# The products of a recurrence tile in three runs by array shape, with rank and table products moved to the end of a step

## The chip, the cores and the metric

One core of one Trainium2 chip. The metric is the device time of one execution in microseconds, the median of several runs.

## The reference

Three stages, one after the other, all in float32:

```
# 1. gated linear attention: 4 batches, 8 heads, 768 steps, 48 features
f = sigmoid(f_logit)
state = f[t] * state + outer(k[t], v[t])
y[t] = q[t] @ state
# 2. mixture of experts on y as 3072 tokens of 384: 8 experts, the best one alone
logits = x @ w_gate + modality_bias[modality_id]
e = argmax(logits); weight = softmax(logits)[e]
out = weight * (relu(x @ w1[e]) @ w2[e])           # 384 -> 1024 -> 384
# 3. gated linear unit, 384 -> 1536 -> 384
out = (sigmoid(x @ w_gate) * (x @ w_val)) @ w_out
```

## The kernel before, in words

Stage 1 goes over 24 tiles of 128 tokens (6 chunks of each of 4 batches, batches in turn, so tile i is chunk i // 4 of batch i % 4). Inside a tile the recurrence is done as matrix products over the 128 tokens; between chunks a state of 48 x 48 per head is carried on. The loop at L1245 has one step per tile and two more; step i works on several tiles at once, and the order in which it calls its parts is the order of every engine's queue (the schedule is by hand). The parts, with the name that the text uses for their products on TensorE:

- **k** (`att_k`, L951): four transposes of the decayed keys of tile i, copied to `kt` by ACT. Not in the last chunk.
- **a** (`att_a`, L962): eight products of 48 rows, keys times queries, into two PSUM banks; `att_m` (L972) masks them on DVE into `am`.
- **c** (`prep_c`, L916): eight products into 64 columns each, the running sums of the log decays of tile i+2. `prep_e` (L929) turns them into `r` and `g` by two exponentials on ACT, and `prep_mul` (L938) makes keys `kT` (DVE) and queries `qT` (POOL, in some tiles DVE) of them. `prep_l` (L907) makes the log decays of tile i+3 on ACT, `limit_f` (L903) limits the logits of tile i+4.
- **x** (`att_x`, L1037): four products that turn the result of tile i-2 back to one token per partition, with the router's logits beside it; ACT copies the rows, DVE sums the logits.
- **u** (`att_u`, L978): eight products of 64 columns, the state's update; DVE carries the state on in `state_steps`, and ACT copies it to `s_blk` in `att_s` (L1002).
- **ys** and **y** (`att_y`, L1009): tile i-1's output. ys are four products of the carried state with the queries (L1015; not in chunk 0, that is tiles 0 to 3), y are eight products of 64 columns of `am` with v (L1021), into the same PSUM bank; ACT copies it to `yT`.

float32 products run in two passes, so the timeline counts two instructions for each of the products of a, c, x, u, ys and y; a transpose is one.

Before the change a step's order on TensorE is k, a, (put), c, (rank), x, u, ys, y. PSUM: `ps_mm` has three banks, which a (two) and c (one) use in turn; `ps_o` has two, which u and yT use in turn; `ps_t` has two for k and x, and one for the routing's small products.

Routing goes by groups of tiles, ROUTE at L42: (0, 4), (4, 4), (8, 4), (12, 4), and so on. When x of a group's last tile is done, a chain of small DVE operations (`route_a`, L243) is put into `chains`; `tick` (L221) issues the next operation of the chains, and is called at places spread over a step; `drain` issues all that are left. One step later `att_r` (L1063) drains, runs the **rank** products (`route_rank`, L267) and puts in a second chain: positions (`route_pos`), counts (`route_cum`) and weights (`route_weight`), and for each tile of the group two marks (`mark`, L306). One step after that `put_table` (L325) drains, and runs the **table** products ("put") of the marks, two for each tile; `store_rows` (L1079) sends the group's rows to memory. With groups of four tiles this is in steps 6, 10, 14, 18 (rank) and 7, 11, 15, 19 (put and store).

SP's queue holds the loads (`load_f`, `load_kq`, `load_v` at the start of a step), the stores of rows, and, around the steps of CONV, loads and stores of the weights that are converted from 64 to 32 bits on ACT and DVE. The loads of a step are for tiles i+3 to i+5.

Stage 2 follows in slots of 256 tokens (`slot32` with float32 products, then `half_slot` and `slot` with split ones), stage 3 after it.

Of the kernel before, what the change touches and what calls it, by code (L numbers as in the profile page):

```python
# [41 lines left out]
ROUTE = ((0, 4), (4, 4), (8, 4), (12, 4), (16, 2), (18, 4), (22, 2))  # L42
CUM = len(ROUTE) % 2
CONV = (3, 7, 11, 15)
GROUP = (0, 6, 1, 2)
STAGED = (3, 7)
PADS = (320, 160, 352, 96)
# [13 lines left out]
def kernel(  # L61
# [181 lines left out]
    def route_a(logits_ps, bias, n, to):  # L243
        shp = [P, n, E]
        lg = small.tile(shp, F32, tag="lg", name="lg")
        nc.vector.tensor_tensor(out=lg, in0=logits_ps, in1=bias, op=ALU.add)
        yield
        mx = small.tile([P, n], F32, tag="mx", name="mx")
        nc.vector.tensor_reduce(out=mx, in_=lg, axis=AX.X, op=ALU.max)
        yield  # L250
        nc.vector.tensor_tensor(out=lg, in0=lg, in1=bc3(mx, shp, 2), op=ALU.subtract)
        ez = small.tile(shp, F32, tag="ez", name="ez")
        nc.scalar.activation(out=ez, in_=lg, func=AF.Exp)
        yield
        sc = small.tile(shp, F32, tag="sc", name="sc")
        w8b = bc3(w8, shp, 1)
        nc.vector.scalar_tensor_tensor(out=sc, in0=lg, scalar=0.0, in1=w8b, op0=ALU.is_ge, op1=ALU.mult)
        yield
        first = small.tile([P, n], F32, tag="first", name="first")
        nc.vector.tensor_reduce(out=first, in_=sc, axis=AX.X, op=ALU.max)  # L260
        yield
        oh = small.tile(shp, BF16, tag="oh", name="oh", bufs=3)
        nc.vector.tensor_tensor(out=oh, in0=w8b, in1=bc3(first, shp, 2), op=ALU.is_equal)
        to.update(oh=oh, ez=ez)
        yield

    def route_rank(oh, c, n, count=False):  # L267
        ps = ps_t.tile([P, n + count, E], F32, tag="lg", name="rank", bufs=1)
# [77 lines left out]
    def route_cum(oh, c, c_new, n):  # L346
        if n > 2:
            total = small.tile([P, E], F32, tag="total", name="total")
            nc.vector.tensor_reduce(out=total, in_=oh.rearrange("p n e -> p e n"), axis=AX.X, op=ALU.add)
            yield  # L350
            nc.vector.tensor_tensor(out=cum[c_new], in0=cum[c], in1=total, op=ALU.add)
            yield
        for j in range(n if n <= 2 else 0):
            nc.vector.tensor_tensor(out=cum[c_new], in0=cum[c if j == 0 else c_new], in1=oh[:, j], op=ALU.add)
            yield
# [650 lines left out]
                at = slice(64 * j, 64 * j + D)  # L1006
                nc.scalar.copy(out=s_blk[b][at, :, at], in_=s_sum[b][at])

    def att_y(i):  # L1009
        c, b = i // B, i % B  # L1010
        (am, _), qT, vt = st.pop(("am", i)), st.pop(("qT", i)), st.pop(("v", i))
        ps = ps_o.tile([P, 4, P], F32, tag="o", name="yT")
        if c:
            for pr in range(4):
                nc.tensor.matmul(  # L1015
                    out=ps[:, pr, :], lhsT=s_blk[b][:, pr, :], rhs=qT[:, pr, :], start=(pr == 0), stop=False
                )
        for pr in range(4):
            for j in range(2):
                h = 2 * pr + j  # L1020
                nc.tensor.matmul(  # L1021
                    out=ps[64 * j:64 * j + 64, pr, :], lhsT=vt[:, h * D:h * D + 64], rhs=am[:, 4 * j + pr, :],
                    start=(c == 0 and pr == 0), stop=(pr == 3),
                )
        yT = ap2.tile([P, 4, P], F32, tag="yT", name="yT")
        nc.scalar.copy(out=yT, in_=ps)
        st["yT", i] = yT
# [35 lines left out]
    def att_r(i):  # L1063

        drain()
        first_i, n = group_of[i]
        c = ROUTE.index((first_i, n)) % 2
        got = st.pop(("oh", first_i))
        oh = got["oh"]
        rank = route_rank(oh, c, n, i == NE - 1)  # L1070
        steps = (
            route_pos(oh, rank, n, first_i, late_at(first_i, n)),
            route_cum(oh, c, 1 - c, n), route_weight(got["ez"], st["rows", first_i], n),
        )
        if i == NE - 1:
            return rank[:, n], steps
        chains.append(turns(*steps))

    def store_rows(i):  # L1079
        first_i, n = group_of[i]  # L1080
        nc.sync.dma_start(
            out=xd[first_i * P:(first_i + n) * P, :].rearrange("(j p) f -> p j f", p=P),
            in_=st.pop(("rows", first_i))[:, 0:n],
        )


    def general(flag):
        with tc.If(flag != 0), ExitStack() as gctx:
# [53 lines left out]
            with tc.For_i(0, NTOK, P) as r0:  # L1142
                row = gp.tile([P, ROW], F32, name="grow", tag="grow")
                nc.sync.dma_start(out=row[:, 0:DM], in_=xg_d[bass.ds(r0, P), :])
                mi = gp.tile([P, 2], I32, name="gmi", tag="gmi")
                nc.sync.dma_start(out=mi, in_=modality[bass.ds(r0, P), :])
                m1 = gp.tile([P, 1], F32, name="gm1", tag="gm1")
                m0 = gp.tile([P, 1], F32, name="gm0", tag="gm0")
                nc.vector.tensor_copy(out=m1, in_=mi[:, 0:1])
                nc.vector.tensor_scalar(out=m0, in0=m1, scalar1=-1.0, scalar2=1.0, op0=ALU.mult, op1=ALU.add)  # L1150
                bi = gp.tile([P, 1, E], F32, name="gbi", tag="gbi")
                nc.vector.tensor_scalar(out=bi[:, 0], in0=bias_b[:, 0, :], scalar1=m0, scalar2=None, op0=ALU.mult)
                nc.vector.scalar_tensor_tensor(
                    out=bi[:, 0], in0=bias_b[:, 1, :], scalar=m1, in1=bi[:, 0], op0=ALU.mult, op1=ALU.add
                )
                pos_i = gp.tile([P, 1], I32, name="gpi", tag="gpi")
                nc.vector.tensor_copy(out=pos_i, in_=pos_f)
                ps = ps_t.tile([P, 3, P], F32, tag="t", name="gxT")
                for c in range(3):
                    nc.tensor.transpose(ps[:, c, :], row[:, c * P:(c + 1) * P], ident)  # L1160
                xt = gp.tile([P, 3, P], F32, name="gxt", tag="gxt")
                nc.vector.tensor_copy(out=xt, in_=ps)
                lg = ps_t.tile([P, 1, E], F32, tag="lg", name="glg", bufs=1)
                for c in range(3):
                    nc.tensor.matmul(out=lg[:, 0], lhsT=xt[:, c, :], rhs=wn[:, c, :], start=(c == 0), stop=(c == 2))
                got = {}
                run(route_a(lg, bi, 1, got))
                oh, ez = got["oh"], got["ez"]
                rank = route_rank(oh, CUM, 1)
                nc.gpsimd.tensor_copy(out=row[:, DM + 1:ROW].bitcast(I32), in_=pos_i)  # L1170
                at = [gp.tile([P, 1], F32, name=f"gat{x}", tag=f"gat{x}") for x in range(2)]
                run(route_pos(oh, rank, 1, to=at))
                g_row = gp.tile([P, 2, HI], F32, name="grw", tag="grw")
                g_place = gp.tile([P, P], F32, name="gpl", tag="gpl")
                nc.vector.tensor_scalar(out=g_row, in0=iota_hi, scalar1=at[1], scalar2=None, op0=ALU.is_equal)
                pos_t = gp.tile([P, 1], F32, name="gpt", tag="gpt")
                nc.vector.tensor_scalar(out=pos_t, in0=pos_f, scalar1=-float(MID), scalar2=None, op0=ALU.add)
                nc.vector.tensor_scalar(
                    out=g_place, in0=iota_lo, scalar1=at[0], scalar2=pos_t, op0=ALU.is_equal, op1=ALU.mult
                )  # L1180
                put = ps_t.tile([HI, 2, P], F32, tag="lg", name="gput", bufs=1)
                for half in range(2):
                    nc.tensor.matmul(
                        out=put[:, half], lhsT=g_row[:, half], rhs=g_place, start=(half == 0), stop=(half == 1)
                    )
                nc.vector.tensor_tensor(out=table, in0=table, in1=put, op=ALU.add)
                nc.vector.tensor_scalar(out=pos_f, in0=pos_f, scalar1=float(P), scalar2=None, op0=ALU.add)
                run(route_cum(oh, CUM, CUM, 1))
                run(route_weight(ez, row.rearrange("p (o f) -> p o f", o=1), 1))
                nc.sync.dma_start(out=xd[bass.ds(r0, P), :], in_=row)  # L1190
# [49 lines left out]
    def ticking(steps):  # L1240
        for _ in steps:
            tick()

    to_store = due = to_put = None
    for i in range(NT + 2):  # L1245
# [9 lines left out]
            load_v(i + 3)  # L1255
        if to_store is not None and to_store != NE - 1:
            store_rows(to_store)
        if i < NT:
            att_k(i)
            att_a(i)  # L1260
# [36 lines left out]
        if i < NT:  # L1297
            state = att_u(i)
            if i == 0:
                keep_warm(1)  # L1300
        if 0 <= i - 1 < NT:
            att_y(i - 1)
        if i == NT - 1:
            gps = ps_t.tile([1, P], F32, tag="lg", name="gps", bufs=1)
# [462 lines left out]
```

## Time and profile before

| what | value |
|---|---|
| median of 3 runs | 879.07 us (875.2 to 879.09) |
| the profiled execution's own time | 878.71 us |
| its span | 877.0 us |
| TensorE busy over the span | 97% |
| DVE, ACT, POOL busy over the span | 54%, 44%, 28% |
| mean granted TensorE clock | 0.991 |

The span runs from the first to the last instruction of the execution; the device time has some 1.7 us around it. Busy shares are means over stages with different limits. The recurrence's loop takes about the first fifth of the span. A step is read from TensorE's k to the next step's k.

### The profile page before, as it was taken

Reading aid. Unit: us, or ns where it says so; the run is one execution under the profiler, and the core shown is the slowest. Engines: PE = TensorE matmul, PEld = TensorE weight load, DVE = VectorE, ACT = ScalarE, POOL = GpSimd, SP = SyncE. Lnnn points to the kernel's source line nnn. Section 1 sums busy time; section 2 is a strip of 40 time slices with the busy share of each in tenths; the row PEclk is TensorE's granted clock in tenths of the full one; section 3 lists DMA queues with packets and bytes.
Section 4 is the critical chain, followed back from the end, with each engine's and each line's share of the span. In section 5 each row is a group of like instructions: output and inputs, shape, how many; then the busy total and the mean of one; then the engine's idle time right before and its main releaser. Section 6 shows DMA issues by size and latency. Waiting matters only on the chain.

```text
span 877.0 us, 15315 instructions
## 1 busy us (share of the span) xinstructions
PE 853.0 (97%) x5802; PEld 762.9 (87%) x5802; DVE 476.8 (54%) x1036; ACT 389.2 (44%) x804; POOL 249.8 (28%) x321
## 2 busy tenths in 40 slices
PE   7999999999999999999999999999999999999995
PEld 6888888777999999999888888888888888888885
DVE  5777778475987979976335334333423433442221
ACT  5866675225866656656432322232322332223222
POOL 5744443113445665564630200020020001002002
PEclk8999999999999999999999999999999999999998
DMA  9566653864989979976202021011012002000000
GB/s 324 177 219 232 217 171 123 332 242 149 336 302 327 330 270 321 333 260 226 80 10 64 27 47 35 1 55 37 18 46 46 19 1 64 10 0 37 1 1 36
DMA packets 52273, 121.15 MB, mean 138 GB/s; under 512 B 21018, under 2 KB 33318, under 8 KB 52192
## 3 DMA queue, kind: packets, MB, share of 16 engines
q1 hardware_dynamic: 47200, 105.10, 35.6%
q0 software_dynamic: 4992, 15.00, 4.8%
q8 instruction: 47, 0.77, 0.4%
q14 instruction: 34, 0.28, 0.1%
HBM read 96.44 MB, written 20.11 MB: 133 GB/s over the span
## 4 chain that ended last, share of the span: by engine, by line
PE 69%; DVE 4%; issue 1%; ACT 1%; POOL 0%; POOLq 0%; DVEq 0%; ACTq 0%
PE gv L1595 11%; PE gv L1596 11%; PE gv L1594 11%; PE y L735 8%; PE o L1619 6%; PE o L1617 6%; PE o L1618 6%; PE h L659 3%; PE h L656 3%; PE h L657 3%; DVE cvt L850 2%; DVE al L389 1%; DVE hl L663 1%; PE xT L403 0%; DVE bl L389 0%
## 5 line engine op out<-in xcount | busy, mean ns | idle before, releaser
L1605 DVE TENSOR_TENSOR sg<-sg,gv 128x256 f32<-128x256 f32 (+1 forms) x145 | 60.2, 415 | 209.3 <-PE gv L1596 209.3
L1606 ACT CAST gh<-sg 128x256 fp32r<-128x256 f32 (+1 forms) x145 | 58.7, 405 | 191.6 <-DVE sg L1605 191.6
L1625 POOL DMA_INDIRECT out_dram<-raw,tok x24 | 23.6, 984 | 375.5 <-ACT raw L1622 369.3
L1607 DVE TENSOR_TENSOR gl<-sg,gh 128x256 fp32r<-128x256 f32 (+1 forms) x145 | 64.3, 443 | 68.2 <-ACT gh L1606 68.2
L1604 ACT ACTIVATE sg<-gv 128x256 f32<-128x256 f32 (+1 forms) x145 | 55.2, 381 | 94.7 <-PE gv L1596 92.6
L393 POOL DMA_INDIRECT xg<-xd,ids x24 | 36.5, 1523 | 62.9 <-PE xT L403 38.9
L662 ACT ACTIVATE hh<-h 128x256 fp32r<-128x256 f32 x80 | 30.9, 386 | 42.7 <-PE h L659 42.0
L663 DVE SCALAR_TENSOR_TENSOR hl<-h,hh 128x256 fp32r<-128x256 f32 x80 | 33.3, 419 | 21.8 <-ACT hh L662 18.2
L1596 PE MATMUL gv<-oddh,al 128*128 128x512 f32 (+1 forms) x120 | 44.3, 369 | 0.0
L1595 PE MATMUL gv<-oddl,ah 128*128 128x512 f32 (+1 forms) x120 | 44.3, 369 | 0.0
L1594 PE MATMUL gv<-oddh,ah 128*128 128x512 f32 (+1 forms) x120 | 44.1, 367 | 0.0
L1596 PE MATMUL gv<-oddh,bl 128*128 128x512 f32 x108 | 42.5, 394 | 0.0
L1596 PE MATMUL gv<-evenh,bl 128*128 128x512 f32 x108 | 42.5, 393 | 0.0
L1595 PE MATMUL gv<-oddl,bh 128*128 128x512 f32 x108 | 42.4, 393 | 0.0
L1595 PE MATMUL gv<-evenl,bh 128*128 128x512 f32 x108 | 42.4, 393 | 0.0
L945 POOL TENSOR_TENSOR qT<-kq,g 128x512 f32<-128x512 f32 x19 | 24.4, 1283 | 62.9 <-ACT g L935 47.8
L1596 PE MATMUL gv<-evenh,al 128*128 128x512 f32 x108 | 42.3, 391 | 0.0
L1595 PE MATMUL gv<-evenl,ah 128*128 128x512 f32 x108 | 42.2, 391 | 0.0
L1594 PE MATMUL gv<-evenh,ah 128*128 128x512 f32 x108 | 42.0, 389 | 0.0
L1594 PE MATMUL gv<-evenh,bh 128*128 128x512 f32 x108 | 42.0, 389 | 0.0
L1594 PE MATMUL gv<-oddh,bh 128*128 128x512 f32 x108 | 42.0, 389 | 0.0
L975 DVE TENSOR_TENSOR am<-a,causal 128x512 f32<-128x512 f32 x48 | 31.2, 683 | 12.5 <-PE a L969 12.5
(365 smaller groups left out, 2487.8 us busy)
## 6 DMA issues: line engine op xcount, KB each, us to landing
raw<-in_w_dram SPq DMA_DIRECT2D x48, 768.0 KB, 5.8
kq<-in_att_kq_dram SPq DMA_DIRECT2D x24, 512.0 KB, 5.4
cvr<-in_w_glu_dram SPq DMA_DIRECT2D x14, 768.0 KB, 7.4
raw<-wd SPq DMA_DIRECT2D x7, 768.0 KB, 5.3
f<-in_att_fv_dram SPq DMA_DIRECT2D x24, 200.0 KB, 5.6
v<-in_att_fv_dram SPq DMA_DIRECT2D x24, 200.0 KB, 2.5
x<-yd SPq DMA_DIRECT2D x12, 386.0 KB, 3.4
xd<-rows SPq DMA_DIRECT2D x5, 772.0 KB
```

Source lines behind the costliest of these rows:

```text
L663: nc.vector.scalar_tensor_tensor(out=hl, in0=ps, scalar=0.0, in1=hh, op0=ALU.max, op1=ALU.subtract)
L735: nc.tensor.matmul(out=ps, lhsT=lhs[:, ts], rhs=rhs[:, fs], start=(g == 0 and part == 0), stop=(g == 7 and part == 2))
L1594: nc.tensor.matmul(out=ps[:, ns], lhsT=hi[:, sl], rhs=xh[:, c, ns], start=(c == 0), stop=False)
L1595: nc.tensor.matmul(out=ps[:, ns], lhsT=hi[:, sl], rhs=xl[:, c, ns], start=False, stop=False)
L1596: nc.tensor.matmul(out=ps[:, ns], lhsT=lo[:, sl], rhs=xh[:, c, ns], start=False, stop=(c == 2))
L1604: nc.scalar.activation(out=sg[:, sl], in_=pss[0][:, to], func=AF.Sigmoid)
L1605: nc.vector.tensor_tensor(out=sg[:, sl], in0=sg[:, sl], in1=pss[1][:, to], op=ALU.mult)
L1606: nc.scalar.copy(out=gh[:, sl], in_=sg[:, sl])
L1607: nc.vector.tensor_tensor(out=gl[:, sl], in0=sg[:, sl], in1=gh[:, sl], op=ALU.subtract)
L1617: nc.tensor.matmul(out=ps, lhsT=gh[:, ts], rhs=hi[:, fs], start=(f == 0), stop=False)
L1618: nc.tensor.matmul(out=ps, lhsT=gh[:, ts], rhs=lo[:, fs], start=False, stop=False)
L1619: nc.tensor.matmul(out=ps, lhsT=gl[:, ts], rhs=hi[:, fs], start=False, stop=(f == 11))
```

## The change

For steps 0 to 17 (GROUPED) the loop has a body of its own, with the same operations in another order. On TensorE: k, then ys of tile i-1 (split off `att_y` as `att_ys`), x of tile i-2; then a; then y of tile i-1, c of tile i+2, u; then, in steps 9, 13 and 17 (PUT), the table products, and in steps 6, 10 and 14 the rank products. The table products thus come three steps behind the rank products, and without a drain. `store_rows` is called at the end of steps 8, 12 and 16. The exponential of the logits is taken out of `route_a` and is issued by `att_r` (`route_exp`), on ACT ahead of `prep_e`. From step 18 on the order is the old one. No product, copy or transfer is added or left out.

```diff
+GROUPED = 17
+PUT = (9, 13, 17)
...
@@ route_a
-        ez = small.tile(shp, F32, tag="ez", name="ez")
-        nc.scalar.activation(out=ez, in_=lg, func=AF.Exp)
...
-        to.update(oh=oh, ez=ez)
+        to.update(oh=oh, lg=lg)
...
+    def route_exp(lg, n):
+        ez = small.tile([P, n, E], F32, tag="ez", name="ez")
+        nc.scalar.activation(out=ez, in_=lg, func=AF.Exp)
+        return ez
...
-    def att_y(i):
+    def att_ys(i):
         c, b = i // B, i % B
-        (am, _), qT, vt = st.pop(("am", i)), st.pop(("qT", i)), st.pop(("v", i))
+        qT = st.pop(("qT", i))
         ps = ps_o.tile([P, 4, P], F32, tag="o", name="yT")
         if c:
             for pr in range(4):
                 nc.tensor.matmul(
                     out=ps[:, pr, :], lhsT=s_blk[b][:, pr, :], rhs=qT[:, pr, :], start=(pr == 0), stop=False
                 )
+        st["y", i] = ps
+
+    def att_y(i):
+        c = i // B
+        (am, _), vt, ps = st.pop(("am", i)), st.pop(("v", i)), st.pop(("y", i))
...
@@ att_r
-        oh = got["oh"]
+        oh, ez = got["oh"], route_exp(got["lg"], n)
...
@@ the loop, behind the loads and the old place of store_rows
+        if i <= GROUPED:
+            att_k(i)
+            if i:
+                att_ys(i - 1)
+            if i >= 2:
+                att_x(i - 2)
+            att_a(i)
+            att_m(i)
+            tick()
+            if i:
+                att_y(i - 1)
+            prep_c(i + 2)
+            state = att_u(i)
+            if i == 0:
+                keep_warm(1)
+            if i in PUT:
+                put_table()
+            if routed is not None:
+                att_r(routed)
+            prep_e(i + 2)
+            prep_l(i + 3)
+            if i in CONV:
+                convert_mask()
+            ticking(state)
+            if i:
+                att_s(i - 1)
+            if i + 1 in PUT:
+                store_rows(i - 5)
+            prep_mul(i + 2)
+            tick(3)
+            limit_f(i + 4)
...
+            continue
...
         if 0 <= i - 1 < NT:
+            att_ys(i - 1)
             att_y(i - 1)
```

The rest of the new body (conversion of weights, the small loads, the bias) is called as at the end of the old one.

## Rows read from the trace of the kernel before

**Rows 1.** The page: span, busy time of the engines, and DVE's group of masks.

```profile
span 877.0 us, 15315 instructions
...
PE 853.0 (97%) x5802; PEld 762.9 (87%) x5802; DVE 476.8 (54%) x1036; ACT 389.2 (44%) x804; POOL 249.8 (28%) x321
...
L975 DVE TENSOR_TENSOR am<-a,causal 128x512 f32<-128x512 f32 x48 | 31.2, 683 | 12.5 <-PE a L969 12.5
```

**Rows 2.** Stretches, steps 3 and 10 to 13: length, busy per engine, clock, DMA share, GB/s.

```profile
27.01:32.27 5.26, 5.26 (x79) 4.53 (x77) 2.80 (x6) 4.27 (x10) 3.05 (x5) 1.00 0.56 181
...
71.24:77.87 6.63, 6.63 (x93) 5.72 (x91) 4.62 (x18) 4.30 (x10) 2.96 (x5) 1.00 0.69 244
77.87:85.54 7.67, 7.41 (x95) 6.36 (x93) 6.27 (x21) 5.11 (x10) 3.10 (x4) 1.00 0.69 227
85.54:92.02 6.48, 6.48 (x86) 5.57 (x85) 4.84 (x9) 4.29 (x9) 3.25 (x4) 1.00 0.46 144
92.02:98.51 6.49, 6.49 (x87) 5.59 (x85) 5.22 (x10) 4.29 (x9) 3.17 (x4) 1.00 0.72 213
```

**Rows 3.** TensorE's timeline, step 12: start, length, line, product, shape, count.

```profile
85.54 0.65 PE L957 MATMUL ktr<-ident,kT 128*128 128x128 f32 x4
86.12 1.16 PE L969 MATMUL a<-qT,kT 48*128 48x128 f32 x16
87.21 1.09 PE L923 MATMUL c<-causal,nl 128*64 128x128 f32 x16
88.24 1.14 PE L1047 MATMUL xtok<-wr,yT 128*128 128x104 f32 x8
89.31 0.67 PE L987 MATMUL u<-v,kt 128*64 128x48 f32 x16
89.91 1.16 PE L1015 MATMUL yT<-qT,s 128*128 128x128 f32 x8
91.00 1.09 PE L1021 MATMUL yT<-am,v 128*64 128x128 f32 x16
```

**Rows 4.** The same timeline cut off inside ys of step 12.

```profile
89.91 0.82 PE L1015 MATMUL yT<-qT,s 128*128 128x128 f32 x5
```

**Rows 5.** TensorE's timeline, u and y of step 3 and the next k.

```profile
30.78 0.67 PE L987 MATMUL u<-v,kt 128*64 128x48 f32 x16
31.28 1.06 PE L1021 MATMUL yT<-am,v 128*64 128x128 f32 x16
32.27 0.66 PE L957 MATMUL ktr<-ident,kT 128*128 128x128 f32 x4
```

**Rows 6.** TensorE's timeline, first expert slots, after the recurrence.

```profile
181.47 0.82 PE L728 MATMUL xT<-ident,xg 128*128 128x128 f32 x6
182.12 1.46 PE L694 MATMUL y<-eh,h 128*128 128x384 f32 x4
...
187.29 0.83 PE L331 MATMUL put<-raw 128*96 128x128 f16 x12
187.96 1.51 PE L694 MATMUL y<-eh,h 128*128 128x384 f32 x4
```

**Rows 7.** ACT's groups, 20 to 130 us: busy, mean ns, idle before and releaser.

```profile
L934 ACT ACTIVATE r<-c 128x512 f32<-128x512 f32 x18 | 10.8, 597 | 18.6 <-PE c L923 18.6
...
L1026 ACT COPY yT<-yT 128x512 f32<-128x512 f32 x17 | 10.0, 585 | 14.0 <-PE yT L1021 14.0
...
L1058 ACT COPY rows<-xtok 128x384 f32<-128x384 f32 x16 | 7.4, 462 | 0.0
```

**Rows 8.** Waits of SP's queue, 20 to 170 us: total, times, longest.

```profile
SPq L900 <- PE yT L1021: 73.6, 18, 5.7
```

**Rows 9.** Waits of DVE in steps 10 to 13: total, times, longest.

```profile
DVE lgs L1051 <- PE xtok L1047: 2.1, 3, 0.8
DVE ss L997 <- PE u L987: 1.7, 4, 0.4
DVE am L975 <- PE a L969: 1.2, 2, 0.9
```

More of the change, by code (lines that the diff above doesn't have):

```diff
@@ L1072, in att_r @@
             route_pos(oh, rank, n, first_i, late_at(first_i, n)),
-            route_cum(oh, c, 1 - c, n), route_weight(got["ez"], st["rows", first_i], n),
+            route_cum(oh, c, 1 - c, n), route_weight(ez, st["rows", first_i], n),
         )
@@ L1167, in general @@
                 run(route_a(lg, bi, 1, got))
-                oh, ez = got["oh"], got["ez"]
+                oh, ez = got["oh"], route_exp(got["lg"], 1)
                 rank = route_rank(oh, CUM, 1)
@@ L1257 @@
             store_rows(to_store)
+        if i <= GROUPED:
[29 more added lines that the diff above has]
+            limit_f(i + 4)
+            if i in CONV:
+                convert_high()
+            if i - 1 in CONV:
+                convert_low()
+            if i - 2 in CONV:
+                convert_store()
+            if i + 2 in CONV:
+                convert_load()
+            if i == 0:
+                load_small()
+            if i == 3:
+                setup_bias()
+            continue
         if i < NT:
```

## The prediction

> **What bounds the kernel now.** I read the page first, then one line per loop step (busy time by stretch), then TensorE's timeline of one plain step, then who waits for whom. The page says that TensorE is busy nearly all the span and that the other engines are not [rows 1]; what is left to find is whether its time is work. One line per step sharpens this: in each step of the recurrence TensorE is busy from end to end at the full granted clock (6.48 of 6.48 us in step 12), DVE never for four steps together, ACT 4.3 us [rows 2]. So the length of a step is TensorE's queue, and nothing else ends last.
>
> The timeline of step 12 shows seven runs, k, a, c, x, u, ys and y, and at each border, that to the next step's k too, the shape of the array changes (the 128\*128, 48\*128 or 128\*64 of a row) [rows 3]. Inside a run one pass follows the other by a fixed pitch (a float32 product has two, and the rows count passes): cutting the ys run after five products shortens its row from 1.16 to 0.82 us, so the pitch is 0.34 / 3 = 0.113 us [rows 3, 4]. Eight cost 0.90, but the run holds TensorE from 89.91 to 91.00, 1.09 us. The rest, 0.19, belongs to its borders.
>
> **What a border costs.** Steps 2 to 4 have no ys, and there u and y, both 128\*64, stand next to each other [rows 5]. Step 3 takes 5.26, step 12 takes 6.48 [rows 2]. Putting ys between u and y therefore costs 1.22, of which 0.90 are its eight passes: two borders cost 0.32, one 0.16. The bounds come from single runs of step 12: x takes 1.07 less 0.90, that is 0.17; k takes 0.58 less 4 times 0.113, that is 0.13; ys 0.19 [rows 3]. I take 0.16, because it is a difference of whole steps with the same neighbours, and keep 0.13 and 0.19.
>
> **The change, part by part.**
>
> *Runs by shape.* A step becomes k, ys, x (128\*128), then a, then y, c, u (128\*64). With ys, seven borders become three: 4 times 0.16 = 0.64 a step. Step i works on ys of tile i-1, which begins with tile 4, so it is there from step 5 on, up to step 17: 13 steps, 13 times 0.64 = 8.3 us. In steps 2 to 4 (no ys) five borders become three: 3 times 0.32 = 1.0. Steps 0 and 1 have three borders before and after: nothing. Sum 9.3; by the bounds 13 times 0.52 plus 0.8 = 7.6, and 13 times 0.76 plus 1.1 = 11.0.
>
> Two neighbours are new. Transposes beside products of the same shape (k, ys) are shown later in the kernel: six transposes hold TensorE from 181.47 to 182.12, 0.108 each, with nothing added before the y products that follow [rows 6]. So no border is hidden there. c after y and u after c are like y after u, which costs nothing [rows 5].
>
> *Table products.* put_table stands between a and c in steps 7, 11 and 15, right behind a drain of the marking work on DVE. Step 11 takes 7.67 against 6.48, so 1.19 us, in which TensorE is busy 7.41 of 7.67 [rows 2]: it waits for the marks. In steps 9, 13 and 17 the marks are older: 19 chain operations against 5 ticks in the routing step and 8 in each of the next two, so the last one is issued a step before the products. Twelve such products take 0.67 us between two 128\*128 runs, 0.056 each and no border [rows 6]; eight cost 0.45, and u to put replaces u to k as the border. Saved: 1.19 less 0.45 = 0.74, three times, 2.2 us. The bounds: 1.7, if u to put cost a border more than u to k; 0, if the marks were late again.
>
> *Rank products.* Between c and x they cost 6.63 less 6.48 = 0.15 [rows 2]; at the end of the step, behind u, they cost the same 0.15, since the border u to k exists anyway. The one-hot they wait for is made in the step before. Nothing.
>
> *The exponential of the logits* goes from the chain to the routing step, ahead of r on ACT; ACT waits for c there in any case, 18.6 us in 18 steps [rows 7]. Nothing; if that wait were gone and it took as long as the copy of rows, 0.46 [rows 7], three routing steps would cost 1.4 us.
>
> *Stores of rows* move on SP's queue from the front of the put step (behind the drain) to the end of the next step, behind that step's loads and ahead of no conversion store. What they wait for, the weights on DVE, is older then; behind them stand the next step's loads, needed one to three steps later. The row buffers are reopened two steps after, by a POOL copy and ACT's row copy. Nothing. The loads of v, which hold up SP until y of an older tile is done [rows 8], come free earlier, since y moves from the end of the step to its middle.
>
> **Sum.** 8.3 + 1.0 + 2.2 = 11.5 us. A plain step should last 6.48 less 0.64 = 5.84. From the profiled execution (878.71 us, span 877.0) that gives 867.2; it lies 0.4 below the median of 879.07, so 867.6 for the median. I say 867.5. After step 17 the program is as before and its waits hang on the steps before it, so the whole 11.5 should reach the end.
>
> **Does cover hold?** In a step of 5.84, from its start: k to 0.45, ys to 1.35, x to 2.25, a from 2.41, y from 3.47, c from 4.35, u from 5.23, end. DVE's two masks of a take 0.68 each [rows 1] and must be done before the next a writes the same banks: due at about 5.0, needed at 5.84 + 2.41 = 8.25, so DVE may run 3.2 us late. Over the cycle of steps 10 to 13 DVE is busy 4.62 + 6.27 + 4.84 + 5.22 = 20.95 us in 27.27 [rows 2]; the new cycle is 4 times 5.84 + 0.15 + 0.45 = 23.96. It fits, with 3.0 to spare.
>
> **The rivals.**
>
> *DVE's waits stay.* DVE's idle time in that cycle is 27.27 less 20.95 = 6.3, and 5.0 of it are waits for x, u and a on TensorE [rows 9]. DVE works in order, and now x, a, u and (by way of c and r) kT are all ends of runs spread over the step. If all 6.3 stayed, the cycle would be 27.27 again and the time 879; if half of what is to go stays, the cycle is 25.6, half the gain is left, and the time is 873. Against it: these waits exist because DVE is early, and it may be 3.2 late. The Trainium skill, in "TensorEngine Tiling (Array Packing)", section "PSUM Bottleneck", says that packing speeds up TensorE but not the reading of PSUM, and that those copies may then be the limit; by it the outcome is this rival, 873 to 879. The busy sums above speak against it so far: DVE has room. Chance 0.08.
>
> *ys waits for ACT* (slower). The yT tiles and the u tiles share two PSUM banks in turn. ys now opens its bank at the head of the queue, 0.45 into a step, and that bank is free only when ACT has copied the yT before it. On time, y ends at 4.35 plus 0.25, the copy takes 0.59 [rows 7], so 5.2, needed at 6.29: 1.1 us of slack. If ACT first works off the rest of its step, 4.29 less copies of 0.59 (yT), 0.59 (kt, of the same size) and 0.46 (rows), that is 2.65 [rows 2, 7], ys waits 1.55 a step with all other products behind it. 13 times (1.55 less 0.64), less 3.2 for the rest, is 8.6 us slower: 888. It decides when ACT is over 1.75 late in every step. Against it: ACT is busy 4.29 of 5.84, and now waits for yT [rows 7], so it is early. Chance 0.03.
>
> *It isn't the shape.* Were the gap one of a new bank or a new accumulation group, seven runs would keep seven gaps and only the table products would gain: 876.9. u to y in step 3 speaks against it, a new bank without a gap [rows 5]. Chance 0.03.
>
> **How the numbers follow.** The forecast has 0.86. Its own range: 7.6 + 1.7 = 9.3 to 11.0 + 2.2 = 13.2 us of gain around 879.07, so 865.9 to 869.8; the three runs before spread over 3.9 us, downwards from the median, which I allow below (to 863). Above I reach to the half of the DVE rival, 872.5. A measurement of this kernel tells about 0.5%, 4.4 us, from no change: faster means below 874.7. Faster 0.90 (the forecast and the better part of the DVE rival), same 0.07, slower 0.03.
>
> **What the profile after would show.** Right: k starts 5.84 apart in plain steps, 4.94 in steps 2 to 4; three borders a step; no idle TensorE time in steps 9, 13 and 17, and these steps near 6.3; DVE's busy share in steps 10 to 13 up to nearly nine tenths, its waits for TensorE shorter. Wrong: a wait of a for am, or of k for kT (DVE is the bound); a wait of ys for ACT's yT; runs y, c, u each with 0.15 of their own (not the shape); a gain in step 18 that is gone by the end of the span.

## The result, and the profile after

The changed kernel takes 869.39 us (median of 5 runs, 867.13 to 870.79) against 879.09 for the kernel before (5 runs, 875.2 to 879.56): ratio 0.9908, interval 0.9884 to 0.9932. It is faster, 9.7 us where 11.5 were forecast, and within the range given. The page of the profiled execution (869.35 us) answers to [rows 1]:

```profile
span 867.6 us, 15306 instructions
...
PE 843.4 (97%) x5802; PEld 762.0 (88%) x5802; DVE 481.2 (55%) x1036; ACT 389.5 (45%) x804; POOL 251.1 (29%) x321
...
L980 DVE TENSOR_TENSOR am<-a,causal 128x512 f32<-128x512 f32 x48 | 31.7, 682 | 7.9 <-PE a L974 7.9
```

TensorE runs the same 5802 instructions and is busy 9.6 us less, at the same share of the span; from the page alone no step that waits can be seen. TensorE's timeline of the plain step 12, which answers to [rows 3], shows the three runs:

```profile
77.48 0.66 PE L962 MATMUL ktr<-ident,kT 128*128 128x128 f32 x4
77.98 1.06 PE L1020 MATMUL yT<-qT,s 128*128 128x128 f32 x8
78.87 1.04 PE L1057 MATMUL xtok<-wr,yT 128*128 128x104 f32 x8
79.84 1.16 PE L974 MATMUL a<-qT,kT 48*128 48x128 f32 x16
80.93 1.09 PE L1031 MATMUL yT<-am,v 128*64 128x128 f32 x16
81.85 1.04 PE L928 MATMUL c<-causal,nl 128*64 128x128 f32 x16
82.73 0.62 PE L992 MATMUL u<-v,kt 128*64 128x48 f32 x16
```

From the start of ys to the start of x is now 0.89 us; with a border behind it, it was 1.09 [rows 3]. y to c and c to u take 0.92 and 0.88; y and c held TensorE for 1.02 and 1.03 with a border behind them [rows 2, 3]. Borders are left only at x to a, a to y and u to the next k.

One line per stretch, as in [rows 2], for step 3 and steps 10 to 13 of the kernel after, then the seam (step 18, the first in the old order) and step 19:

```profile
25.56:30.46 4.90, 4.90 (x81) 4.62 (x77) 2.43 (x5) 4.30 (x10) 2.67 (x3) 1.00 0.71 208
...
65.31:71.71 6.40, 6.17 (x93) 5.66 (x92) 5.86 (x16) 5.71 (x14) 3.43 (x4) 1.00 0.90 315
71.71:77.48 5.77, 5.77 (x90) 5.50 (x86) 4.20 (x14) 4.04 (x10) 3.13 (x3) 1.00 0.88 313
77.48:83.28 5.80, 5.80 (x89) 5.52 (x85) 5.61 (x12) 4.09 (x9) 3.09 (x3) 1.00 0.90 293
83.28:89.91 6.63, 6.54 (x96) 6.02 (x93) 6.60 (x15) 4.12 (x10) 3.27 (x3) 1.00 0.13 36
...
114.51:123.04 8.53, 7.20 (x94) 5.97 (x92) 8.11 (x25) 6.64 (x15) 4.71 (x6) 1.00 0.67 219
123.04:130.62 7.58, 7.38 (x95) 6.32 (x93) 6.08 (x28) 4.29 (x9) 1.49 (x3) 1.00 0.38 131
```

Plain steps are as forecast (5.8). Steps 9, 13 and 17 (table products, 6.63 to 6.64) and 10 and 14 (rank products, 6.40) are longer than 6.28 and 5.91, which they take where nothing waits (experiment 5 below), and TensorE stands idle in steps 10 and 13; step 18 lasts 8.53 where it lasted 6.63. The whole difference of the two profiled executions, from the k of one step to the k of another:

| stretch | before | after | difference | forecast |
|---|---|---|---|---|
| start to the k of step 2 | 21.75 | 20.66 | -1.09 | 0 |
| steps 2 to 4 | 15.78 | 14.70 | -1.08 | -1.0 |
| steps 5 to 17 | 88.24 | 79.15 | -9.09 | -10.5 |
| step 18 | 6.63 | 8.53 | +1.90 | 0 |
| step 19 to the end | 744.60 | 744.56 | -0.04 | 0 |

The first line is not the change's. Steps 0 and 1 of the kernel before, of the kernel after, and of the third experiment below (ys or x are in none of them):

```profile
9.60:21.75 12.15, 10.02 (x123) 8.66 (x123) 7.99 (x14) 5.41 (x11) 3.42 (x13) 0.72 1.03 364
```

```profile
10.54:20.66 10.12, 9.25 (x123) 8.29 (x123) 6.05 (x12) 5.10 (x10) 2.10 (x7) 0.83 0.97 326
```

```profile
10.81:19.39 8.58, 7.70 (x123) 6.85 (x123) 6.04 (x12) 4.98 (x10) 2.10 (x7) 1.00 1.02 347
```

The column behind POOL is the granted clock: 0.72, 0.83 and 1.00. The same 123 instructions take 12.15, 10.12 and 8.58 us by how much of them ran at 1.2 instead of 2.4 GHz. The order does not do it: experiment 1, with the old order of these steps and a granted clock of 1.00, takes 8.59. In the profiled executions of this document steps 0 and 1 take 8.58 to 13.59 us, so in what follows parts of the recurrence are compared from the k of step 2 on.

Where do steps 9, 10 and 18 lose? TensorE's timeline of after in step 14 and in step 18 (in brackets the idle time and its releaser):

```profile
90.74 1.16 PE L1020 MATMUL yT<-qT,s 128*128 128x128 f32 x8 [0.23 <-ACT yT L1036]
...
115.05 1.75 PE L974 MATMUL a<-qT,kT 48*128 48x128 f32 x16
117.46 1.09 PE L928 MATMUL c<-causal,nl 128*64 128x128 f32 x16 [0.67 <-ACT nl L918]
119.11 0.19 PE L278 MATMUL rank<-oh,before 128*128 128x32 bf16 x1 [0.56 <-DVE oh L263]
```

In steps 10 and 14 ys waits for ACT's copy of the yT before it. The waits up to 170 us have it for TensorE's weight loads (PEld) five times, in steps 9, 13 and 17 too, where ys starts 0.75 behind k instead of 0.50:

```profile
ACT rows L1068 <- DVE lgs L1061: 15.3, 11, 2.4
...
PEld yT L1020 <- ACT yT L1036: 1.9, 5, 0.5
```

ACT's timeline at the end of step 9 shows why that copy is late:

```profile
62.12 0.59 ACT L964 COPY kt<-ktr 128x512 f32<-128x512 f32 x1
65.12 0.48 ACT L1068 COPY rows<-xtok 128x384 f32<-128x384 f32 x1 [2.42 <-DVE lgs L1061]
65.50 0.59 ACT L1036 COPY yT<-yT 128x512 f32<-128x512 f32 x1
```

Ahead of the yT copy in ACT's queue stands the copy of the rows, and it waits 2.42 us for DVE's sum of the logits (lgs), which the program puts first on the same PSUM tile. DVE's timeline at that place:

```profile
53.74 0.68 DVE L951 SCALAR_TENSOR_TENSOR kT<-r,kq 128x512 f32<-128x512 f32 x1
54.34 1.24 DVE L303 TENSOR_TENSOR hi<-df,lo 128x4 f32<-128x4 f32 x1
...
60.82 1.28 DVE L312 TENSOR_SCALAR row<-iota_hi,hi 128x192 f16<-128x192 bf16 x1
...
63.05 0.94 DVE L866 SCALAR_TENSOR_TENSOR raw<-raw,raw 128x768 int32<-128x768 int32 x1
64.03 0.96 DVE L869 SCALAR_TENSOR_TENSOR raw<-raw 128x768 f32<-128x768 f32 x1
64.91 0.18 DVE L1061 TENSOR_REDUCE lgs<-xtok 128x8 f32<-128x32 f32 x1
```

and POOL's products for qT at the same time:

```profile
53.71 1.84 POOL L950 TENSOR_TENSOR qT<-kq,g 128x512 f32<-128x512 f32 x1 [2.89 <-ACT g L940]
...
60.50 1.53 POOL L950 TENSOR_TENSOR qT<-kq,g 128x512 f32<-128x512 f32 x1 [3.64 <-issue]
```

x ended near 61.4, DVE came to its sum at 64.91: it was late with marks and weight conversion, by an amount that does not matter to TensorE's next a (68.11).

### The profile page after: what moved, and what is told of

It is laid out like the page before. It is cut to its first block, busy times and chain, and to the rows that moved or that the text cites. A ratio compares the mean times of both kernels' runs of the same rounds, so it can differ in the third digit from the quotient of the medians.

```text
span 867.6 us, 15306 instructions
## 1 busy us (share of the span) xinstructions
PE 843.4 (97%) x5802; PEld 762.0 (88%) x5802; DVE 481.2 (55%) x1036; ACT 389.5 (45%) x804; POOL 251.1 (29%) x321
## 4 chain that ended last, share of the span: by engine, by line
PE 68%; DVE 5%; issue 2%; ACT 1%; POOL 0%; DMA 0%; POOLq 0%; DVEq 0%; ACTq 0%
PE gv L1650 11%; PE gv L1651 11%; PE gv L1649 11%; PE y L740 8%; PE o L1674 6%; PE o L1672 6%; PE o L1673 6%; PE h L664 3%; PE h L661 3%; PE h L662 3%; DVE cvt L855 2%; DVE al L394 1%; DVE hl L668 1%; PE xT L408 0%; DVE bl L394 0%
## 5 line engine op out<-in xcount | busy, mean ns | idle before, releaser
L950 POOL TENSOR_TENSOR qT<-kq,g 128x512 f32<-128x512 f32 x19 | 28.6, 1507 | 54.4 <-issue 34.5
```

## The experiments

Lengths below are from TensorE's k to k; "2 to y" is from the k of step 2 to the start of the last pass of the recurrence's last y: 142.81 us in the kernel before, 134.53 after.

**1. The table products alone.** The kernel before with only this moved (no drain, stores at steps 8, 12, 16):

```diff
+PUT = (9, 13, 17)
...
-        if to_store is not None and to_store != NE - 1:
+        if to_store is not None and 12 <= to_store != NE - 1:
             store_rows(to_store)
...
-        if to_put and to_put < NE - 1:
+        if to_put and 12 <= to_put < NE - 1:
             drain()
             put_table()
... (behind u, ahead of ys)
+        if i in PUT:
+            put_table()
...
+        if i + 1 in PUT:
+            store_rows(i - 5)
```

> The old order of the products, with the table products alone moved to steps 9, 13 and 17 and no drain ahead of them. If my split of the gain is right, steps 7, 11 and 15 lose the 1.17 us that they have over a plain step, and steps 9, 13 and 17 get 0.45 us each: 2.2 us less than before, 876.9 by the median, with plain steps still at 6.48. If the gain of the table products came only from the new order, 879.

Measured: 876.37 us (10 runs) against 879.24 (13 runs), ratio 0.9974, interval 0.9958 to 0.9991. Steps 7, 11 and 15 last 6.49, steps 9, 13 and 17 6.92. From the k of step 2 to that of step 18: 101.83 instead of 104.03, 2.20 us. The term of the table products stands by itself.

**2. Two borders back.** The kernel after with x between c and u:

```diff
             att_ys(i - 1)
-            if i >= 2:
-                att_x(i - 2)
...
             prep_c(i + 2)
+            if i >= 2:
+                att_x(i - 2)
             state = att_u(i)
```

> The changed kernel with x put back between c and u, so that a step has five borders of shape and not three. If a border costs 0.16 to 0.17 us by shape, every step from 2 to 17 is 0.33 longer: step 3 5.23, a plain step 6.12; the copy of yT is then ahead of the copy of rows on ACT, so ys should not wait in steps 9 and 10. Sum 16 times 0.33 less 2.0: 872.7. If the gap is not of the shape, a plain step stays at 5.79 and the time falls to about 867.4.

Measured: 871.4 us (4 runs), ratio 0.9923, interval 0.99 to 0.9947. Plain steps last 6.14 (+0.35), step 3 5.25 (+0.35). Two borders cost 0.35, with the same products, tiles and banks: it is the shape, 0.17 each on the mean. The step of the table products shows the late copy here too: step 9 lasts 6.98, c waiting for ACT's nl.

**3. Is it only ys's bank?** The kernel after with x ahead of ys, by which the yT bank is opened 0.9 us later:

```diff
-            if i:
-                att_ys(i - 1)
             if i >= 2:
                 att_x(i - 2)
+            if i:
+                att_ys(i - 1)
```

> The changed kernel with x ahead of ys, both of the same shape. If ys waits only because its PSUM bank is still being copied by ACT, the 0.97 us of x ahead of it cover the wait of 0.25 to 0.36 and the restart behind it: step 9 6.25 instead of 6.64, step 10 5.95 instead of 6.40, five such steps, 2.0 us less, 867.4; step 18 stays at 8.5. If ACT or DVE is the bound there, the wait turns up at the next product (a for am, c for nl, u for kt) and the time stays at 869.4.

Measured: 868.05 us (4 runs), ratio 0.9873, interval 0.9856 to 0.9889. Steps 9 and 10 last 6.64 and 6.41, nothing is won there (2 to y 134.72). In the profiled executions the whole gain is the start at full clock shown above: the k of step 2 comes at 19.39 instead of 20.66. That the lower median has the same cause is not shown. The waits of this kernel up to 120 us:

```profile
ACT rows L1068 <- DVE lgs L1061: 15.3, 11, 2.4
...
PE xtok L1057 <- ACT yT L1036: 0.4, 2, 0.2
```

The wait went from ys to x with the releaser unchanged: x reads what that same copy writes. A bank that is needed later does not help; the copy has to come earlier.

**4. The copy of the rows ahead of DVE's sum**, for all tiles:

```diff
         out, src = rows[:, j, 0:DM]..., ps[:, :, 0:2 * D]
-        if NE <= i:
-            nc.scalar.copy(out=out, in_=src)
+        nc.scalar.copy(out=out, in_=src)
         nc.vector.tensor_reduce(out=lg[:, j], ...)
...
-        if i < NE:
-            nc.scalar.copy(out=out, in_=src)
```

> The changed kernel with ACT's copy of the rows issued ahead of DVE's sum of the logits of the same PSUM tile. Theory: the copy waits for that sum, DVE is 2.4 us late in steps 8 and 9, and so ACT comes late to yT. Then ACT is on time, ys waits nowhere, steps 9 and 10 are 6.25 and 5.95, and in step 18 c no longer waits for nl (0.67): 2.0 + 0.7 less, 866.7. Rival: ACT is late because of its own work (the mask of 0.9 us in steps 7, 11, 15); then ys waits as before and the time stays at 869.4.

Measured: 868.02 us (4 runs), ratio 0.9882, interval 0.9858 to 0.9906; 2 to y 132.92. Steps 9, 13, 17 last 6.28 and steps 10, 14 5.91, with no wait of ys left; step 18 lasts 7.49 instead of 8.53, and c in it no longer waits for nl. From step 19 on 1.5 us are lost: there DVE's sum now waits for ACT, and the table products 0.38 and rank 0.58 for DVE.

**5. The same up to tile 15 only:**

```diff
-        if NE <= i:
+        if i <= 15 or NE <= i:
...
-        if i < NE:
+        if 15 < i < NE:
```

> As the run with the copy of rows first, but for the tiles up to 15 alone, whose x is in the new order. In that run step 19 and the ones behind it lost 1.5 us, since DVE's sum of the logits waited for ACT's copy in the old order of steps 18 and 19. Now steps 9 and 10 stay at 6.28 and 5.91, step 18 at about 7.5, and step 19 goes back to 7.58: 131.4 us from step 2 to the last y, 3.1 less than the changed kernel, 866.3 by the median. Rival: the 1.5 us are DVE work that was only put off; then it is 132.9 again.

Measured: 866.56 us (4 runs, 865.96 to 866.63) against 879.33 (7 runs), ratio 0.9858, interval 0.983 to 0.9886; 2 to y 131.45. Its ACT timeline in step 9 beside that of after:

```profile
61.23 0.58 ACT L964 COPY kt<-ktr 128x512 f32<-128x512 f32 x1
61.72 0.49 ACT L1060 COPY rows<-xtok 128x384 f32<-128x384 f32 x1
63.31 0.58 ACT L1036 COPY yT<-yT 128x512 f32<-128x512 f32 x1 [1.11 <-PE yT L1031]
```

and its DVE timeline:

```profile
59.72 1.23 DVE L314 TENSOR_SCALAR place<-iota_lo,lo,iota_t 128x128 f16<-128x128 bf16 x1
...
64.66 0.18 DVE L1061 TENSOR_REDUCE lgs<-xtok 128x8 f32<-128x32 f32 x1
```

DVE is as late as before (64.66), but in steps 9 to 17 nothing on TensorE's path waits for it: ACT copies the rows at 61.72 and then waits for TensorE instead of for DVE. All 3.1 us of "2 to y" come from there: 2.06 in steps 9 to 17, 1.04 in step 18.

**6. DVE undisturbed.** The product qT goes from POOL to DVE for all tiles; the rows' copy stays as in the kernel after:

```diff
-VEC_Q = (0, 1, 2, 20, 21)
+VEC_Q = tuple(range(22))
```

> The changed kernel with the product for qT on DVE in all tiles, not on POOL. Theory: DVE is late in steps 7 to 9 because its small operations stand still beside POOL's product for qT (a subtraction of 4 elements takes 1.24 us in place of 0.16); without POOL's product DVE saves some 1.2 us a step and pays 0.7 for its own, is less late, and ys waits less: steps 9 and 10 between 6.3 and 6.5, 5.95 and 6.3. Rival: those long times are waits of another kind; then DVE only gets 0.7 us more a step, is later still, and steps 9 and 10 grow beyond 6.64 and 6.40.

Measured: 873.35 us (one run). Steps 9 and 10 last 6.28 and 5.91 here too, step 18 7.26. DVE's groups in steps 5 to 16 of the kernel after (35.36 to 107.88 us), and of this one in the same stretch of time (its steps begin 3.1 us later):

```profile
L312 DVE TENSOR_SCALAR row<-iota_hi,hi 128x192 f16<-128x192 bf16 x9 | 5.5, 608 | 0.1
...
L303 DVE TENSOR_TENSOR hi<-df,lo 128x4 f32<-128x4 f32 x3 | 3.7, 1238 | 0.0
...
L356 DVE TENSOR_TENSOR cum<-cum,total 128x8 bf16<-128x8 bf16 x3 | 2.5, 844 | 0.0
```

```profile
L312 DVE TENSOR_SCALAR row<-iota_hi,hi 128x192 f16<-128x192 bf16 x9 | 2.9, 320 | 0.1
...
L356 DVE TENSOR_TENSOR cum<-cum,total 128x8 bf16<-128x8 bf16 x3 | 0.5, 150 | 0.0
L303 DVE TENSOR_TENSOR hi<-df,lo 128x4 f32<-128x4 f32 x3 | 0.4, 149 | 0.0
```

Without a qT on POOL the small operations take their usual time, DVE is early enough although it has twelve products of 0.68 us more, and the wait is gone as well. So the chain is shown at both of its ends: a late DVE, and ACT's copy behind it. From the k of step 2 to the last y this kernel gains 3.3 us on after (131.19). The time is no better, for two reasons. Its start had more time at 1.2 GHz (the k of step 2 comes at 23.79, 3.1 us later than in after). And 4.3 us come back after the recurrence: near 165 us TensorE's cnt (the count of tokens per expert) waits 3.4 us where it waited 0.7, and 3.4 us at 1.2 GHz follow.

**7. The early copy and qT on DVE together** (5 and 6):

> Rows first for tiles up to 15 and qT on DVE in all tiles, the order of the changed kernel. If both repair one and the same wait (ACT late behind DVE), steps 9 and 10 stay at 6.28 and 5.91, step 18 at 7.3 to 7.5, and the time at 866.5: no gain over rows first alone. If DVE's stalls cost something of their own, step 18 falls below 7.2.

Measured: 870.24 us (4 runs), ratio 0.9894, interval 0.9875 to 0.9914. No gain was forecast (866.5), and it is slower. The recurrence gains 0.6 us on number 5 (2 to y 130.89), all of it in step 18: that lasts 6.94, below the 7.2 of the forecast, so DVE's stalls do cost something of their own at the seam. The wait of 3.4 us is there again, at the same place:

```profile
163.45 0.18 PE L373 MATMUL cnt<-cum,ones 128*128 128x8 bf16 x1 [3.36 <-DVEq L1098]
```

It waits for DVE's sequencer at a branch. Why that is later when DVE has more products is open.

**8. The seam one step on**, with the store of that group behind step 19's drain:

```diff
-GROUPED = 17
+GROUPED = 18
...
+            if i == GROUPED:
+                to_put = routed
...
+            store_rows(to_put)
```

> The changed kernel with step 18 in the new order too (its store of rows then behind the drain of step 19). Theory: the 1.9 us that step 18 loses belong to the change of order, since the old order calls c and the rank products earlier in a step than ACT and DVE have nl and the one-hot ready. Then step 18 takes 5.8 + 0.15 and the wait of ys of some 0.4, 6.3 instead of 8.53, and step 19, whose drain waits for DVE anyway, some 0.5 more than 7.58: 1.7 us less from step 2 to the last y (134.5 to 132.8). Rival: DVE is behind by the conversions of steps 15 and 16 whatever the order; then step 18 stays above 7.5.

Measured: 871.63 us (one run). Step 18 lasts 6.40: the 8.53 were the change of order, not tile 18. But step 19 then meets marks that are not ready:

```profile
120.56 1.16 PE L974 MATMUL a<-qT,kT 48*128 48x128 f32 x16
123.93 1.58 PE L336 MATMUL put<-place,row 128*96 128x128 f16 x8 [2.21 <-DVE place L314]
125.44 1.98 PE L928 MATMUL c<-causal,nl 128*64 128x128 f32 x16
127.34 2.04 PE L1057 MATMUL xtok<-wr,yT 128*128 128x104 f32 x8
```

After 2.2 us without work the clock is at 1.2 GHz for 10.2 us: c takes 1.98 us instead of 1.09. 2 to y is 139.01, worse than after; how much of that the clock makes differs by execution (see the next one).

**9. Seam and early copy.** The edit of 8, and that of 5 up to tile 16:

```diff
-        if NE <= i:
+        if i <= 16 or NE <= i:
```

> Copy of rows first for the tiles up to 16, and step 18 in the new order: the two repairs together. If they add up: 131.4 less 1.5 for step 18 (7.5 to 5.95), plus up to 0.5 in step 19: 129.9 to 130.4 us from step 2 to the last y, 865 by the median. If both repair the same wait, 131.4 and 866.

Measured: 868.18 us (4 runs, 865.21 to 871.63), ratio 0.9878, interval 0.9835 to 0.9922. Step 18 lasts 5.91, the wait of 2.21 in step 19 stays, here with 3.4 us at 1.2 GHz behind it; 2 to y 133.85, outside both forecasts.

**10. As 9, with the last table products at the end of step 19** and all marks issued early in that step:

```diff
-        if to_put and to_put < NE - 1:
+        if to_put and to_put < NE - 1 and i != NE + 1:
...
-        tick()
+        tick(8 if i == NE + 1 else 1)
...
+        if i == NE + 1:
+            drain()
+            put_table()
+            store_rows(to_put)
```

> Step 18 in the new order, rows first for tiles up to 16, and the table products of tiles 12 to 15 moved from the front of step 19, where they waited 2.2 us for DVE's marks, to its end, ahead of the rank products of tiles 16 and 17; eight ticks in place of one behind the masks of step 19, so that the marks are made in DVE's free time. Theory: step 18 5.91, no wait of 2.2 and so no fall of the clock behind it; from step 2 to the last y 131.45 less 1.6 (step 18) less up to 0.7 in step 19: 129.2 to 130.5. Rival: the marks and the one-hot of tiles 16 and 17 stand in one row on DVE, and the wait only moves to the end of step 19: 131 or more.

Measured: 866.14 us (4 runs, 863.71 to 869.3), ratio 0.9865, interval 0.9836 to 0.9894. The wait is 1.17 us, of rank for DVE's sum of the table, and in the profiled run 3.4 us at 1.2 GHz follow; 2 to y 131.70: the rival (131 or more) came true. Its lowest run is the fastest of all, but number 5 is as good in the median and simpler: it is the version to keep.

## Why the prediction held, and where it was off

**Borders: right, a little small.** 0.16 was taken, 0.17 measured: 6.48 to 5.80 in step 12 is 0.68 for four, and experiment 2 gives 0.35 for two. It is a mean: the single runs of step 12 got shorter by nothing (a, which keeps its borders) up to 0.20 (ys). Steps 2 to 4 gave 1.08 for 1.0. Where nothing waits (experiment 5) steps 5 to 17 last 77.1 us (91.80 from the k of step 2 to that of step 18, less 14.70 for steps 2 to 4), where 13 times 5.84, three times 0.45 (table) and three times 0.15 (rank) make 77.7. The Trainium skill, in "TensorEngine Tiling (Array Packing)", section "Key Properties", says that changing the tiling mode drains TensorE; the runs show a cost at such changes, 0.17 us each on the mean, and not by itself that it is a drain. The rival that the gap is not the shape's is out: c and u open new banks behind y without a gap.

**Table products: right** (2.2 forecast, 2.20 in experiment 1). **Rank, exponential and stores: nothing, right up to step 17.** Rank adds 0.14 to 0.17 to its step, as before. The stores of rows in steps 8, 12 and 16 wait for nothing on DVE. SP's queue now stands up to 7.2 us at a store of converted weights, behind the late DVE (2.7 before); between 20 and 130 us no engine's wait for a load is on record.

**Cover: the step that failed first.** "DVE may run 3.2 us late" was worked out for one reader alone, a's banks. DVE was about 2.4 us late for ACT, within that bound, and a did not wait in steps 5 to 17. But a second engine stood behind DVE: ACT's copy of the rows, ahead of the yT copy. The rival "ys waits for ACT" named the very wait (its 1.1 us of slack and 1.75 of lateness), but saw ACT late by its own work, in every step; it was late by DVE's, in the steps of the marks. A wait of ys for yT is among the prediction's own signs of being wrong. Cost: 2.06 us, by experiment 5. The Trainium skill, in "TensorEngine Tiling (Array Packing)", section "PSUM Bottleneck", says that the copies out of PSUM may become the limit; here TensorE waited for such a copy in five steps, but not because copies are slow: with the same copies in another order (experiment 5) none of these waits is left.

**DVE's busy sum was low for this kernel.** 20.95 us a cycle were carried over from the kernel before; in steps 10 to 13 it is 5.86 + 4.20 + 5.61 + 6.60 = 22.27, in a cycle of 24.60. Other operations meet POOL's qT: hi takes 1238 ns where it took 163, cum 844 where 153; in the kernel before it was lg that took 587. But the sum is not what makes DVE late: in experiment 5 it is 20.95 again, in a cycle of 23.75, and DVE comes to its sum of the logits as late (64.66). A busy sum over four steps does not show where in them the work piles up. The rival "DVE's waits stay" is out: its waits for TensorE in steps 10 to 13 fell from 5.0 us [rows 9] to 2.2 (1.4 for u, 0.8 for a).

**The seam: the step that failed next.** "After step 17 the program is as before and its waits hang on the steps before it, so the whole 11.5 should reach the end" is where 1.90 us were given back. An old step asks for a 0.6 us after its k and for c 1.7 after, a new one 2.4 and 4.4 after. So at the seam a follows the a before it by 4.46 us (110.59 to 115.05) instead of a whole step, c by 4.85 with its wait, and rank stands in the middle instead of at the end. Each was asked for too early: a before DVE had masked the a before it, whose banks it needs (its row stretched to 1.75), c 0.67 before ACT's nl, rank 0.56 before DVE's one-hot. 1.04 of it goes with the copy of the rows (experiment 5): c no longer waits. The other 0.86 goes with the order, since step 18 lasts 5.91 in the new one (experiments 9 and 10). But 0.55 of this 0.86 also goes in the old order, when DVE has no qT on POOL beside it (experiment 7, 6.94): only rank still waits, 0.29. So it takes both, a late DVE and an order that asks early; that the shorter distance is what the order does is argued, not shown by a run of its own.

By terms: -11.1 in steps 5 to 17 without waits, +2.06 for the yT copy, +1.90 at the seam, -1.08 in steps 2 to 4, and -1.09 of clock at the start, which belongs to this pair of executions: 9.3 of the span's 9.4. Without the start the change is worth 8.3 us in this pair, less than the 9.3 of the prediction's lower bounds. The medians differ by 9.7, and that this is nearer to 11.5 is in part luck of the start: the one run of after with a mean clock of 0.997 takes 867.13, a run of the kernel before at 0.997 (beside experiment 1) 875.18, 8.05 more.

## What to carry to other kernels

Products of like array shape belong side by side: it saves a price per border (0.17 us on the mean here), and a cut of the timeline inside a run shows it. When a step is shortened, lateness of an engine must be followed to everything that waits for it, not only to the bottleneck: an operation that needs nothing from the late engine but a turn at the same tile should go first. Where two orders of a loop meet, work out for each product how much sooner it is asked for than a full step later.

## What the runs showed of the hardware that was not expected

- A DVE operation on four elements per partition took 1238 ns while POOL made a 128x512 product of two inputs, and 149 to 163 ns without it. In the lines above hi ends at 55.58 and POOL's product at 55.55. The Trainium skill, in "SBUF — State Buffer", section "SBUF: two separate sides", says that DVE and GpSimd (POOL here) share a pair of ports that is locked for a whole instruction; the trace agrees, and moving POOL's product away ended it (experiment 6).
- TensorE's clock fell to 1.2 GHz behind an idle time of 3.4 us (experiments 6 and 7), of 2.2 us (experiments 8 and 9) and in one run of 1.17 us (experiment 10); waits of 0.67 and 0.56 us in step 18 of the kernel after left it at 2.4 GHz. Behind the same 2.21 us it stayed low for 10.2 us in experiment 8 and for 3.4 in experiment 9.
- The first steps ran from none to 10.2 us at 1.2 GHz in different profiled executions, without regard to the order of their products (experiment 1, in the old order, none; the kernel before 6.8), and the k of step 2 came between 19.4 and 23.8 us. The spread of the runs is of the same size (4.4 us for the kernel before); that this is its cause is not shown.
